# Sparse attention feeding a routed feed-forward layer: per-head-pair phases replaced by 128-query tiles over all heads, with a hand-written order

## The chip, the cores and the metric

The program runs on one core of a Trainium2 chip. A core has five engines that run at the same time and wait for each other through semaphores: TensorE (PE, matrix products; its weight loads are shown apart as PEld), VectorE (DVE), ScalarE (ACT), GpSimd (POOL) and SyncE (SP). Transfers between the large memory (DRAM) and the core's SBUF are issued by an engine's queue, here POOL and SP, and are carried out by 16 DMA engines. The metric is device time in microseconds (us) from the first to the last instruction; lower is better.

## What is computed

There are 4 batches, 8 heads, 768 positions and 64 values per head. Attention is sparse: a query sees the keys less than 16 positions away, and one summary for each of the 24 blocks of 32 keys (the maximum of the keys; the mean of the values). The heads' results stand side by side as 512 values per position. Then, for each batch, one of eight feed-forward experts is picked from the mean over positions, and only that expert's weights are used.

```python
k_sum = k.reshape(B, H, nb, 32, D).max(axis=3)
v_sum = v.reshape(B, H, nb, 32, D).mean(axis=3)
mask_l = np.abs(pos[:, None] - pos[None, :]) < 16
scores_s = scale * einsum('bhsd,bhnd->bhsn', q, k_sum) + np.log(32)
a = softmax(concat([where(mask_l, scale * q @ k.T, -1e9), scores_s]))
x = (a @ concat([v, v_sum])).transpose(0, 2, 1, 3).reshape(B, S, 512)
e_idx = argmax(x.mean(axis=1) @ w_gate, axis=1)
for e in range(8):
    mask = e_idx == e
    out[mask] = gate_w[mask] * (relu(x[mask] @ w1[e]) @ w2[e])
```

## The kernel before

Queries are taken in 12 blocks of 64 (`NJ`). A block needs 96 keys (its own 64 and 16 on either side) and the 24 summaries: 120 rows, which are the contraction of the second product. The work of a batch has these phases:

- `load_inputs(b)` (L75 to L121) issues the loads from POOL's queue: q and k in 128-position groups, 6 transfers each (L79, L83), alternating, and then v in overlapping windows of 96 rows, one transfer per head (L102). The overlap is read from DRAM again. Data is cast from float32 to bfloat16 on the way.
- `phase_T` (L245), for each of four head pairs: transposes of q and k on PE, the key blocks with their halos and block maxima on DVE (L260 to L285), sums of v over blocks on PE (L290), and a transfer on SP's queue that copies these sums into 24 rows of `vblk` for all 12 blocks (L301).
- `phase_S_head` (L308), for each head: scores (L321) into PSUM, exponential on ACT (L329), mask on DVE (L332), product with `vblk` (L339), reciprocal and scaling on DVE (L347, L348).
- `phase_X` (L355): transposes of the result; ACT's copy also adds up the positions for the gate (L359).
- The gate (L379 to L422): logits, the largest of eight, its index loaded into a register of POOL; then POOL issues the loads of that expert's weights, w1 in two halves (L426) and w2 in one piece (L433).
- The feed-forward of a batch (`moe_groups`, L177) is cut into 22 pieces: hidden layer by 128 features (L185, L199, relu L192, L206), output by 128 positions (L213, L221, written out at L222). They are handed out between the heads of the next batch.

The order in which an engine's instructions stand is chosen by a scheduler from priorities, within what the data allows; only the order of issue in the source guides it. The loads of batch b+1 are issued at the start of batch b (L240). On PE, ACT and DVE an instruction that waits holds up all behind it on that engine. PSUM has four pools of two banks each.

Of the kernel before, what the change touches and what calls it, by code (L numbers as in the profile page):

```python
# [12 lines left out]
FP32 = mybir.dt.float32  # L13
# [7 lines left out]

EMIT_ORDER = "T_all_first"
# [3 lines left out]
def kernel(  # L26
# [22 lines left out]
    NR = KW + NB  # L49
# [3 lines left out]
    NFT = F // 128  # L53
    SCALE = 1.0 / math.sqrt(D)
    KPAD = 16

    const_pool = ctx.enter_context(tc.tile_pool(name="const", bufs=1))

    ld_pool = ctx.enter_context(tc.tile_pool(name="ld", bufs=2))
    vb_pool = ctx.enter_context(tc.tile_pool(name="vb", bufs=2))  # L60
    pair_pool = ctx.enter_context(tc.tile_pool(name="pairp", bufs=6))
    head_pool = ctx.enter_context(tc.tile_pool(name="headp", bufs=8))
    xt_pool = ctx.enter_context(tc.tile_pool(name="xtp", bufs=2))
    moe_pool = ctx.enter_context(tc.tile_pool(name="moe", bufs=2))
    misc_pool = ctx.enter_context(tc.tile_pool(name="misc", bufs=2))

    tps_pool = ctx.enter_context(tc.tile_pool(name="tps", bufs=2, space=bass.MemoryType.PSUM))
    sc_pool = ctx.enter_context(tc.tile_pool(name="sc", bufs=2, space=bass.MemoryType.PSUM))
    ops_pool = ctx.enter_context(tc.tile_pool(name="ops", bufs=2, space=bass.MemoryType.PSUM))
    mps_pool = ctx.enter_context(tc.tile_pool(name="mps", bufs=2, space=bass.MemoryType.PSUM))  # L70


    v_off = v.offset

    def load_inputs(b):  # L75
        q_nat = ld_pool.tile([128, NG, H, D], BF16, name="q_nat")
        k_nat = ld_pool.tile([128, NG, H, D], BF16, name="k_nat")
        for g in range(NG):
            nc.gpsimd.dma_start(  # L79
                q_nat[:, g, :, :],  # L80
                q[b, :, g * 128 : (g + 1) * 128, :].rearrange("h p d -> p h d"),
            )
            nc.gpsimd.dma_start(  # L83
                k_nat[:, g, :, :],
                k[b, :, g * 128 : (g + 1) * 128, :].rearrange("h p d -> p h d"),
            )
        vblk = vb_pool.tile([NR, NP, NJ, 2, D + 1], BF16, name="vblk")
        nc.vector.memset(vblk[0:KW, :, :, :, D : D + 1], 1.0)
        for h in range(H):
            prc = h // 2  # L90
            hh = h % 2
            first_tensor_head = b == 0 and h == 0
            last_tensor_head = b == B - 1 and h == H - 1
            j_lo = 1 if first_tensor_head else 0
            j_hi = NJ - 1 if last_tensor_head else NJ
            base_elem = v_off + ((b * H + h) * S + (QB * j_lo - KPAD)) * D
            src = bass.AP(
                tensor=v.tensor,
                offset=base_elem,
                ap=[[D, KW], [QB * D, j_hi - j_lo], [1, D]],  # L100
            )
            nc.gpsimd.dma_start(vblk[0:KW, prc, j_lo:j_hi, hh, 0:D], src)  # L102
            if first_tensor_head:
                nc.gpsimd.dma_start(
                    vblk[KPAD:KW, prc, 0, hh, 0:D],
                    v[b, h, 0 : KW - KPAD, :],
                )
                nc.gpsimd.dma_start(
                    vblk[0:KPAD, prc, 0, hh, 0:D],
                    v[b, h, 0:KPAD, :],  # L110
                )
            if last_tensor_head:
                nc.gpsimd.dma_start(
                    vblk[0 : KW - KPAD, prc, NJ - 1, hh, 0:D],
                    v[b, h, S - (KW - KPAD) : S, :],
                )
# [355 lines left out]
```

## Time and profile before

| what | value |
|---|---|
| runs of the kernel, median (lowest to highest) | 242.04 us (241.69 to 242.19) |
| profiled execution: span from the first to the last instruction | 242.9 us |
| PE, DVE, ACT, POOL busy | 177.5, 105.9, 89.4, 85.6 us |
| first product on PE | at 21.4 us |
| loads of an expert's weights issued (four gates) | at 67.7, 115.1, 162.2 and 207.3 us |
| bytes read from and written to DRAM | 38.8 MB and 6.3 MB |

The profiled execution is known by its span alone; it lies 0.8 us above the median of the three runs. [...] A stage begins here where an expert's weights have landed and the hidden layer starts, since nothing of that batch's feed-forward can start before.

### The profile page before, as it was taken

The numbers are of one execution on the slowest core, as the hardware profiler recorded it, in microseconds if no ns is written. First come the engines' busy times: TensorE is split into PE (matmuls) and PEld (weight loads), VectorE is DVE, ScalarE is ACT, GpSimd is POOL, SyncE is SP. The second block draws the span as 40 slices with busy tenths as digits, with TensorE's granted clock in tenths as the row PEclk, the third lists the DMA queues.
The fourth block names the chain that finished last, engine by engine and source line by source line (L and its number), as shares of the span: only waits on it lengthen the run. The fifth ranks groups of instructions, "written<-read, shape, count | busy, mean of one in ns | idle before, by whom it ended". The sixth has DMA issues, their size and how long they took to land.

```text
span 242.9 us, 4351 instructions
## 1 busy us (share of the span) xinstructions
PE 177.5 (73%) x1712; PEld 106.2 (44%) x1712; DVE 105.9 (44%) x369; ACT 89.4 (37%) x193; POOL 85.6 (35%) x106
## 2 busy tenths in 40 slices
PE   0002257599959999788299999974999994098993
PEld 0002155477734555357145554652455443044441
DVE  1005999666597444028945340397354404000000
ACT  2000001463233465172045753800657437035432
POOL 8999999348185247016900000021000000300000
PEclk9999999655685999999869999997799998559999
DMA  8999999999969999939999504219900131793033
GB/s 52 149 132 96 126 145 129 106 125 137 114 102 186 152 103 148 212 135 109 160 171 137 17 3 167 91 31 185 170 15 0 46 149 68 101 186 61 0 131 130
DMA packets 104548, 27.18 MB, mean 112 GB/s; under 512 B 93264, under 2 KB 101456, under 8 KB 104528
## 3 DMA queue, kind: packets, MB, share of 16 engines
q0 software_dynamic: 95744, 19.40, 139.6%
q1 hardware_dynamic: 8784, 7.51, 11.8%
q8 instruction: 13, 0.21, 0.4%
q14 instruction: 7, 0.06, 0.1%
HBM read 38.81 MB, written 6.29 MB: 186 GB/s over the span
## 4 chain that ended last, share of the span: by engine, by line
PE 53%; DMA 19%; DVE 8%; POOL 8%; ACT 6%; issue 4%; POOLq 1%; ACTq 0%
PE hps L185 16%; PE hps L213 13%; DMA w_sb<-in_moe_w_dram 9%; PE hps L199 6%; PE sc L321 6%; PE ops L339 5%; DMA out_dram<-o_sb 5%; DMA vblk<-vsum_aug 5%; PE vsps L290 4%; POOL vblk L102 3%; ACT o_sb L221 2%; POOL q_nat L79 2%; POOL k_nat L83 2%; PE xps L358 2%; ACT hT_sb L192 1%
## 5 line engine op out<-in xcount | busy, mean ns | idle before, releaser
L185 PE MATMUL hps<-xT_b,w_sb 128*128 128x512 bf16 x128 | 41.3, 438 | 12.6 <-DMA w_sb<-in_moe_w_dram 11.4
L329 ACT ACTIVATE aT<-sc 128x512 bf16<-128x512 f32 x64 | 29.2, 490 | 51.6 <-PE sc L321 51.4
L213 PE MATMUL hps<-w_sb,hT_sb 128*128 128x512 bf16 x192 | 43.8, 379 | 2.1 <-ACT o_sb L221 1.9
L332 DVE TENSOR_TENSOR aT<-aT,mask_full 120x512 bf16<-120x512 bf16 x64 | 20.9, 346 | 52.3 <-ACT aT L329 52.2
L426 POOL DMA_DIRECT2D w_sb<-in_moe_w_dram x8 | 6.3, 791 | 91.3 <-DVE grec L410 83.3
L192 ACT ACTIVATE hT_sb<-hps 128x512 bf16<-128x512 f32 x32 | 19.1, 597 | 50.4 <-PE hps L185 50.4
L248 PE MATMUL qps<-identb,q_nat 128*128 128x128 bf16 x96 | 10.2, 246 | 32.3 <-POOL identb masks.py:199 21.4
L102 POOL DMA_DIRECT2D vblk<-in_v_dram x32 | 28.8, 938 | 12.0 <-PE ops L339 10.7
L213 PEld LDWEIGHTS <-hT_sb 128*128 128x128 bf16 x192 | 17.9, 98 | 23.0 <-issue 2.9
L221 ACT ACTIVATE o_sb<-hps,gcol 128x512 f32<-128x512 f32 x24 | 16.4, 688 | 28.8 <-PE hps L213 19.9
L321 PE MATMUL sc<-qT,kTaug 64*128 64x64 bf16 x384 | 23.1, 203 | 4.9 <-ACT aT L329 2.6
L83 POOL DMA_DIRECT2D k_nat<-in_k_dram x24 | 21.8, 907 | 13.3 <-DMA vblk<-in_v_dram 8.0
L79 POOL DMA_DIRECT2D q_nat<-in_q_dram x24 | 22.0, 918 | 7.2 <-DMA vblk<-in_v_dram 5.4
L321 PEld LDWEIGHTS <-kTaug 64*128 64x128 bf16 x384 | 16.4, 102 | 17.1 <-issue 15.0
L199 PE MATMUL hps<-xT_b,w_sb 128*128 128x256 bf16 x128 | 23.3, 298 | 0.0
L185 PEld LDWEIGHTS <-w_sb 128*128 128x128 bf16 x128 | 12.2, 107 | 23.9 <-DMA w_sb<-in_moe_w_dram 12.0
L248 PEld LDWEIGHTS <-q_nat 128*128 128x128 bf16 x96 | 7.2, 110 | 33.6 <-issue 27.8
L290 PE MATMUL vsps<-vblk,bindw 96*24 96x130 bf16 x192 | 18.7, 252 | 3.1 <-DVE bindw L174 2.6
L339 PE MATMUL ops<-vblk,aT 120*64 120x65 bf16 x384 | 16.6, 213 | 2.6 <-DMA vblk<-vsum_aug 1.5
L348 DVE TENSOR_TENSOR xs_pair<-ops,rv 128x384 bf16<-128x384 f32 x32 | 17.7, 554 | 0.4
L199 PEld LDWEIGHTS <-w_sb 128*128 128x128 bf16 x128 | 12.7, 107 | 9.5 <-issue 3.6
L339 PEld LDWEIGHTS <-aT 120*64 120x64 bf16 x384 | 11.4, 118 | 11.4 <-DVE aT L332 6.4
(69 smaller groups left out, 179.7 us busy)
## 6 DMA issues: line engine op xcount, KB each, us to landing
out_dram<-o_sb SPq DMA_DIRECT2D x24, 256.0 KB
vblk<-in_v_dram POOLq DMA_DIRECT2D x30, 144.0 KB, 8.2
w_sb<-in_moe_w_dram POOLq DMA_DIRECT2D x8, 512.0 KB, 6.6
w_sb<-in_moe_w_dram POOLq DMA_DIRECT2D x4, 1024.0 KB, 12.6
q_nat<-in_q_dram POOLq DMA_DIRECT2D x24, 128.0 KB, 6.0
k_nat<-in_k_dram POOLq DMA_DIRECT2D x24, 128.0 KB, 6.1
vblk<-vsum_aug SPq DMA_DIRECT2D x16, 73.1 KB
vblk<-in_v_dram POOLq DMA_DIRECT2D x2, 132.0 KB, 11.1
```

Source lines behind the costliest of these rows:

```text
L79: nc.gpsimd.dma_start(q_nat[:, g, :, :], q[b, :, g * 128 : (g + 1) * 128, :].rearrange("h p d -> p h d"),)
L83: nc.gpsimd.dma_start(k_nat[:, g, :, :], k[b, :, g * 128 : (g + 1) * 128, :].rearrange("h p d -> p h d"),)
L102: nc.gpsimd.dma_start(vblk[0:KW, prc, j_lo:j_hi, hh, 0:D], src)
L185: nc.tensor.matmul(hps1, lhsT=w1_sb[:, dt, ft * 128 : (ft + 1) * 128], rhs=xT_b[:, dt, 0:512], start=(dt == 0), stop=(dt == NDT - 1),)
L192: nc.scalar.activation(hT_sb[:, ft, 0:512], hps1, ACT.Relu)
L199: nc.tensor.matmul(hps2[:, 0 : S - 512], lhsT=w1_sb[:, dt, ft * 128 : (ft + 1) * 128], rhs=xT_b[:, dt, 512:S], start=(dt == 0), stop=(dt = ...
L213: nc.tensor.matmul(o_ps[:, 0:DM], lhsT=hT_sb[:, ft, st * 128 : (st + 1) * 128], rhs=w2_sb[:, ft, :], start=(ft == 0), stop=(ft == NFT - 1),)
L221: nc.scalar.activation(o_sb, o_ps[:, 0:DM], ACT.Copy, scale=gcol[:, 0:1])
L290: nc.tensor.matmul(vs_ps, lhsT=bindw[0:KW, j, :], rhs=vblk[0:KW, pr, j, :, :], start=(j == 0), stop=(j == NJ - 1),)
L321: nc.tensor.matmul(sc[0:128, cs], lhsT=kTaug[rs, j, :], rhs=qT[rs, QB * j : QB * (j + 1)], start=True, stop=True, tile_position=(hh * D, 0),)
L329: nc.scalar.activation(aT[:, j0 * QB : j1 * QB], sc[:, 0:ncols], ACT.Exp, scale=SCALE)
L339: nc.tensor.matmul(ops[(j % 2) * QB : (j % 2 + 1) * QB, j // 2, 0 : D + 1], lhsT=aT[0:NR, QB * j : QB * (j + 1)], rhs=vblk[0:NR, pr, j, hh ...
```

## The change

The kernel is written anew around tiles of 128 queries over all eight heads, and the scheduler is switched off: every engine's instructions stand as the source issues them. What differs:

- `vblk` and the key blocks `kaug` are two static tiles each, used in turn. v is loaded without overlap into 64 rows, two transfers of four heads each; the halo rows are copied from there by SP transfers (`halo`); the sums are copied into their 24 rows by DVE.
- Key blocks are made for all heads at once; the block maximum is a tree of DVE maxima, no longer one reduction.
- Scores, exponential, mask, second product and scaling are done for 128 queries and 8 heads in one go; one ACT instruction covers 1024 columns. Heads alternate between the upper and lower half of PE's rows.
- PSUM has two pools: two banks for transposes and three tiles of two banks (`big`) for everything else.
- w1 is loaded in four pieces, w2 in two; the hidden layer uses 384 columns per product.
- The order of loads, attention steps and feed-forward chunks is a list at the end. `weave` deals out steps among chunks.

```diff
-        vblk = vb_pool.tile([NR, NP, NJ, 2, D + 1], BF16, name="vblk")
...
-            nc.gpsimd.dma_start(vblk[0:KW, prc, j_lo:j_hi, hh, 0:D], src)
...
-    loaded = {0: load_inputs(0)}
-    identb = const_pool.tile([128, 128], BF16, name="identb")
-    make_identity(nc, identb)
...
+    ctx.enter_context(tc.manual_schedule())
...
+    tps_pool = ctx.enter_context(tc.tile_pool(name="tps", bufs=2, space=bass.MemoryType.PSUM))
+    big_pool = ctx.enter_context(tc.tile_pool(name="big", bufs=3, space=bass.MemoryType.PSUM))
...
+    def load_v(b):
+        vb = vblks[b % NV]
+        for a in range(2):
+            hs = slice(4 * a, 4 * a + 4)
+            nc.gpsimd.dma_start(
+                vb[0:QB, hs, :, 0:D].rearrange("p h j d -> p (h j) d"),
+                v[b, hs].rearrange("h (j p) d -> p (h j) d", p=QB),
+            )
+    def halo(b):
+        vb = vblks[b % NV]
+        for a in range(2):
+            hs = slice(4 * a, 4 * a + 4)
+            nc.sync.dma_start(
+                vb[R_PRE : R_PRE + HALO, hs, 1:NJ, :],
+                vb[QB - HALO : QB, hs, 0 : NJ - 1, :],
+            )
...
+    load_k(0)
+    identb = const.tile([128, 128], BF16, name="identb")
+    make_identity(nc, identb)
...
+    load_v(0)
+    load_q(0)
...
+    def V_sum(b):
+        def f():
...
+            for j in range(NJ):
+                for pr in range(NP):
+                    nc.tensor.matmul(
+                        vs_ps[BLK * pr : BLK * (pr + 1), :],
+                        lhsT=bind[:, j, :],
+                        rhs=vb[0:QB, 2 * pr : 2 * pr + 2, j, :],
...
+            nc.vector.tensor_copy(vs_sb.rearrange("p h c -> p (h c)"), vs_ps)
+            for pr in range(NP):
+                nc.vector.tensor_copy(
+                    vb[R_SUM:NR, 2 * pr : 2 * pr + 2, :, :],
...
+        for c in range(4):
+            fs = slice(c * (F // 4), (c + 1) * (F // 4))
+            nc.gpsimd.dma_start(w1_sb[:, :, fs], w1_src[:, :, fs])
...
+    def q_steps(b):
+        steps = [T_q(b, 0), T_q(b, 1)]
+        for g in range(NG + 2):
+            if g < NG:
+                steps.append(S_tile(b, g))
+            if g + 2 < NG:
+                steps.append(T_q(b, g + 2))
+            if 0 <= g - 1 < NG:
+                steps.append(O_tile(b, g - 1))
+            if 0 <= g - 2 < NG:
+                steps.append(X_tile(b, g - 2))
+        return steps
...
+    run(k_steps(0))
+    run(v_steps(0))
+    run(q_steps(0))
+    load_k(1)
+    edges(1)
+    gate(0)
+    load_v(1)
+    load_q(1)
+    load_k(2)
+    run(k_steps(1))
+    gate_col(0)()
+    weave(Hs(0), v_steps(1) + q_steps(1)[0:3])
+    weave(Os(0), q_steps(1)[3:])
+    gate(1)
+    load_v(2)
+    load_q(2)
+    load_k(3)
+    h1 = Hs(1)
+    weave(h1, k_steps(2) + v_steps(2) + q_steps(2)[0:3])
+    gate_col(1)()
+    weave(Os(1), q_steps(2)[3:])
+    load_v(3)
+    load_q(3)
+    gate(2)
+    weave(Hs(2), k_steps(3) + v_steps(3) + q_steps(3)[0:3])
+    gate_col(2)()
+    weave(Os(2)[0:6], q_steps(3)[3:])
+    gate(3)
+    run(Os(2)[6:])
+    gate_col(3)()
+    run(Hs(3))
+    run(Os(3))
```

`k_steps` are three `T_k` (transposes of k) and `K_rest` (halos, maxima); `T_q` transposes q, `S_tile` makes scores, exponential and mask, `O_tile` the second product and scaling, `X_tile` the transposes of the result and the sum over positions for the gate; `Hs` are the eight chunks of the hidden layer, `Os` the twelve half chunks of the output.

Three places show how instructions moved. The first is the start of POOL's queue in the kernel before; `L79` and `L83` are loads of q and k, `L102` of v (two small transfers for the first rows are left out).

```order
L83 DMA k_nat<-in_k_dram 128x8x64
L102 DMA vblk<-in_v_dram 96x11x64
...
L102 DMA vblk<-in_v_dram 96x12x64 x7
masks.py:197 MEMSET identb 128x128
L140 ISA
L140 IOTA it_u 96x768
masks.py:199 AFFINE_SELECT identb<-identb 128x128
```

In the changed kernel POOL's queue starts so (`L87` loads k or q, `L102` v).

```order
L87 DMA k_nat<-in_k_dram 128x8x64 x6
masks.py:197 MEMSET identb 128x128
masks.py:199 ISA
masks.py:199 AFFINE_SELECT identb<-identb 128x128
L124 IOTA it_u 96x64
L126 IOTA it_p 128x1
L128 IOTA it_b 64x384
L102 DMA vblk_84<-in_v_dram 64x48x64 x2
L87 DMA q_nat<-in_q_dram 128x8x64 x6
```

The identity, which every transpose needs, stood behind 12 loads of q and k and the ten transfers of v; it now stands behind the six loads of k, and v and q come after it.

The second place is POOL's queue at the first gate (`TENSOR_LOAD` waits for the expert's index). Before, v of batch 1, q and k of batch 2 and two heads of v of batch 2 stood ahead of it:

```order
L83 DMA k_nat<-in_k_dram 128x8x64
L102 DMA vblk<-in_v_dram 96x12x64 x2
L417 TENSOR_LOAD ix_691
L417 ISA x2
L426 ISA
L426 DMA w_sb<-in_moe_w_dram 128x4x512
...
L433 DMA w_sb<-in_moe_w_dram 128x8x512
L102 DMA vblk<-in_v_dram 96x12x64 x6
```

Now only k of batch 1 stands ahead of it, and v and q of batch 1 come behind the weights:

```order
L87 DMA k_nat<-in_k_dram 128x8x64 x6
L370 TENSOR_LOAD ix_601
L370 ISA x2
L383 ISA
L383 DMA w_sb<-in_moe_w_dram 128x4x256
...
L386 DMA w_sb<-in_moe_w_dram 128x4x512
L102 DMA vblk_85<-in_v_dram 64x48x64 x2
L87 DMA q_nat<-in_q_dram 128x8x64 x6
L87 DMA k_nat<-in_k_dram 128x8x64 x6
```

What moved is the load of v and q of the next batch: from ahead of the gate's wait to behind the weights. At the second gate it stands the same way; ahead of the third gate v and q of batch 3 are already issued.

The third place is on PE, where the sums of v over blocks stand. Before (`L290`, here those of batch 2), they lie among the transposes of q and k (`L248`, `L256`) around the gate's own products (`L412`), ahead of the hidden layer:

```order
L290 LDWEIGHTS bindw
L290 MATMUL vsps<-vblk,bindw 24x130
L248 LDWEIGHTS q_nat
L248 MATMUL qps<-identb,q_nat 128x128
...
L412 MATMUL gps<-grec,ones_row 128x1
L248 LDWEIGHTS q_nat
L248 MATMUL qps<-identb,q_nat 128x128
...
L185 LDWEIGHTS w_sb
L185 MATMUL hps<-xT_b,w_sb 128x512
```

In the changed kernel the sums of batch 1 (`L243`) stand behind the second of eight chunks of the hidden layer (`L424`) of batch 0:

```order
L424 MATMUL hps<-xT,w_sb 128x384
L243 LDWEIGHTS bind
L243 MATMUL vsps<-vblk_85,bind 32x132
...
L243 LDWEIGHTS bind
L243 MATMUL vsps<-vblk_85,bind 32x132
L424 LDWEIGHTS w_sb
L424 MATMUL hps<-xT,w_sb 128x384
```

Six chunks of the hidden layer, and everything after, now stand behind a product that needs v of the next batch.

## Rows read from the trace of the kernel before

**Rows 1.** The chain that ended last, in order of time: start, length, what.

```profile
36.80 11.35 DMA vblk<-vsum_aug
...
67.66 5.27 DMA w_sb<-in_moe_w_dram
...
115.05 6.21 DMA w_sb<-in_moe_w_dram
...
162.16 5.40 DMA w_sb<-in_moe_w_dram
...
207.29 5.39 DMA w_sb<-in_moe_w_dram
```

**Rows 2.** Timeline of the start: start, length, engine, line; idle time before, its end.

```profile
1.38 1.01 POOL L79 DMA_DIRECT2D q_nat<-in_q_dram  x1 [0.81 <-POOLq L456]
...
21.44 0.80 PE L248 MATMUL qps<-identb,q_nat 128*128 128x128 bf16 x6 [21.44 <-POOL identb masks.py:199]
```

**Rows 3.** Stretches: length; PE, PEld, DVE, ACT, POOL busy; clock, DMA, GB/s.

```profile
16.00:25.00 9.00, 1.44 (x12) 1.28 (x12) 3.82 (x4) 0.00 (x0) 9.00 (x14) 1.00 4.04 104
28.00:36.00 8.00, 4.62 (x41) 4.10 (x41) 7.94 (x23) 0.00 (x0) 8.00 (x10) 1.00 3.47 146
70.00:80.00 10.00, 8.41 (x56) 4.50 (x53) 7.54 (x29) 3.71 (x8) 6.15 (x8) 0.66 1.19 192
...
212.70:218.00 5.30, 5.27 (x17) 2.46 (x18) 0.00 (x0) 1.58 (x3) 0.00 (x0) 0.50 1.19 182
```

**Rows 4.** The chain again: its pieces on PE that give prices.

```profile
48.18 0.54 PE ops L339 x12
48.72 0.75 PE sc L321 x12
...
59.12 1.95 PE vsps L290 x17
...
86.58 0.35 PE ops L339 x12
...
89.05 0.44 PE hps L199 x4
...
108.33 0.44 PE xps L358 x6
...
228.17 10.53 PE hps L213 x48
```

**Rows 5.** Groups by line and shape: count, busy us, mean ns; idle before.

```profile
L79 POOL DMA_DIRECT2D q_nat<-in_q_dram x24 | 22.0, 918 | 7.2 <-DMA vblk<-in_v_dram 5.4 <-DMA w_sb<-in_moe_w_dram 0.9 <-POOLq L456 0.8
...
L348 DVE TENSOR_TENSOR xs_pair<-ops,rv 128x384 bf16<-128x384 f32 x32 | 17.7, 554 | 0.4
...
L266 DVE TENSOR_REDUCE kmx<-kTp 128x24 bf16<-128x768 bf16 x16 | 15.2, 947 | 0.0
...
L332 DVE TENSOR_TENSOR aT<-aT,mask_full 120x512 bf16<-120x512 bf16 x32 | 13.3, 414 | 50.1 <-ACT aT L329 49.9
L359 ACT ACTIVATE xT_b<-xps 128x768 bf16<-128x768 bf16 x16 | 12.9, 821 | 5.5 <-PE xps L358 5.3
...
L252 DVE COPY qT<-qps 128x768 bf16<-128x768 bf16 x16 | 8.4, 527 | 3.0 <-PE qps L248 3.0
L274 DVE COPY kTaug<-kTp 128x768 bf16<-128x768 bf16 x16 | 7.0, 436 | 0.0
...
L347 DVE RECIPROCAL rv<-ops 128x6 f32<-128x6 f32 x32 | 6.3, 196 | 17.5 <-PE ops L339 17.3
L281 DVE COPY kTaug<-kmx 128x288 bf16<-128x288 bf16 x16 | 5.5, 346 | 0.0
```

**Rows 6.** Timeline of the last gate, and of the end of the wait for weights.

```profile
205.41 0.15 DVE L396 COPY lg<-lgps 1x8 f32<-1x8 f32 x1 [0.29 <-PE lgps L394]
...
207.29 1.49 POOL L426 DMA_DIRECT2D w_sb<-in_moe_w_dram  x2 [42.36 <-DVE grec L410]
...
212.73 0.61 PE L185 MATMUL hps<-xT_b,w_sb 128*128 128x512 bf16 x1 [5.42 <-DMA w_sb<-in_moe_w_dram]
```

More of the change, by code (lines that the diff above doesn't have):

```diff
@@ L42 @@
     F = moe_w1.shape[2]
-    assert D == 64 and S % 128 == 0 and H % 2 == 0
+    assert D == 64 and S == 768 and H == 8
     QB = 64
-    KW = 96
+    HALO = 16
     BLK = 32
@@ new lines, with gate @@
+    gcols = {}
+    wts = {}
+    def gate(b):
+        pooled = small.tile([128, NP], FP32, name="pooled")
+        nc.vector.tensor_reduce(out=pooled, in_=red[b], axis=AX.X, op=ALU.add)
+        lgps = tps_pool.tile([128, 512], FP32, name="lgps", tag="tps")
+        for pr in range(NP):
+            nc.tensor.matmul(
+                lgps[0:1, 0:E],
+                lhsT=pooled[:, pr : pr + 1],
+                rhs=wg_sb[:, pr, :],
+                start=(pr == 0),
+                stop=(pr == NP - 1),
+            )
+        lg = small.tile([1, E], FP32, name="lg")
@@ new lines, in gate @@
+        for c in range(2):
+            fs = slice(c * (NFT // 2), (c + 1) * (NFT // 2))
+            nc.gpsimd.dma_start(w2_sb[:, fs, :], w2_src[:, fs, :])
+        negm = small.tile([1, 1], FP32, name="negm")
+        nc.vector.tensor_scalar(
+            out=negm, in0=mx8[0:1, 0:1], scalar1=-1.0 / S, scalar2=None, op0=ALU.mult
+        )
+        ex8 = small.tile([1, E], FP32, name="ex8")
+        se = small.tile([1, 1], FP32, name="se")
+        nc.scalar.activation(
+            out=ex8, in_=lg, func=ACT.Exp, bias=negm[0:1, 0:1], scale=1.0 / S, accum_out=se
+        )
@@ new lines, with H_chunk, f @@
+    hTs = {}
+    o_open = {}
+    def H_chunk(b, ft):
+        def f():
+            if ft == 0:
+                hTs[b] = xpool.tile([128, NFT, S], BF16, name="hT")
+            w1_sb = wts[b][0]
+            hps = big_pool.tile([128, 2, 512], FP32, name="hps", tag="big")
+            for half in range(2):
+                for dt in range(NDT):
+                    nc.tensor.matmul(
+                        hps[:, half, 0:HB],
+                        lhsT=w1_sb[:, dt, ft * 128 : (ft + 1) * 128],
+                        rhs=xT[b][:, dt, half * HB : (half + 1) * HB],
+                        start=(dt == 0),
+                        stop=(dt == NDT - 1),
+                    )
+            nc.scalar.activation(
+                hTs[b][:, ft, :].rearrange("p (u s) -> p u s", u=2),
+                hps[:, :, 0:HB],
+                ACT.Relu,
+            )
+        return f
@@ new lines, in O_chunk, with f @@
+    def O_chunk(b, st, part):
+        def f():
+            w2_sb = wts[b][1]
+            if part == 0:
+                o_open[b] = big_pool.tile([128, 2, 512], FP32, name="ops2", tag="big")
+            o_ps = o_open[b][:, 0, :]
+            for ft in range(4 * part, 4 * part + 4):
+                nc.tensor.matmul(
+                    o_ps,
+                    lhsT=hTs[b][:, ft, st * 128 : (st + 1) * 128],
+                    rhs=w2_sb[:, ft, :],
+                    start=(ft == 0),
+                    stop=(ft == NFT - 1),
+                )
+            if part == 1:
+                o_sb = opool.tile([128, DM], FP32, name="o_sb")
+                nc.scalar.activation(o_sb, o_ps, ACT.Copy, scale=gcols[b][:, 0:1])
+                nc.sync.dma_start(out[b, st * 128 : (st + 1) * 128, :], o_sb)
+        return f
@@ new lines, in run, with weave @@
+    def run(steps):
+        for s in steps:
+            s()
+    def weave(main, fill):
+        n, m = len(main), len(fill)
+        done = 0
+        for i, s in enumerate(main):
+            s()
+            want = (m * (i + 1)) // n
+            while done < want:
+                fill[done]()
+                done += 1
+    run(k_steps(0))
[8 more added lines that the diff above has]
+    run(k_steps(1))
```

562 lines of the change are left out of this document (242 added, 320 removed).

## Prediction

> **What bounds the kernel now.** I read the chain of waits first. It names the end of one wait per batch, the landing of that batch's expert weights, at 72.93, 121.26, 167.56 and 212.68 us (start plus length in [rows 1]). I cut the span of 242.9 us there: a start of 72.9, stages of 48.3, 46.3 and 45.1, and an end of 30.2. The chain also shows what made the start long: 11.35 us until the sums of v had been copied to their place, so that the first second product ran at 48.18 ([rows 1, 4]). The timeline says why it began late at all: POOL issues from 1.38 us, but PE's first transpose is at 21.44 and waited for the identity, which stands behind 22 loads on POOL ([rows 2]). At the other end, from the logits to the issue of the weights is 1.9 us and from the issue to the first product 5.4 ([rows 6]).
>
> The stretches give the transfer rates, counted as bfloat16 is written (an expert is 2.1 MB, v, q or k of a batch 0.79 MB). While v of batch 0 is moved, into 96 partitions, it is 104 GB/s; while q and k are, into 128, it is 146 with POOL issuing all the time; weights come at 182 to 192 ([rows 3]). Weights and v go through one queue in order, so these times add up.
>
> **The start.** POOL: 1.38 us and six loads of k at 0.9 ([rows 2, 5]) end at 6.8. Identity and three small iotas stand in no row of that size; nothing is the lower bound, the four instructions at 1 us each (as one load issue) the upper; I take 2.3, to 9.1. Then v. Its fixed part, from issue to first use, is what the first half of w1 needs beyond its 512 KB at 192 GB/s: 5.4 less 2.7 is 2.7 ([rows 3, 6]). The bytes take 5.4 us at the rate of q and k, 7.6 at that of v before; the new transfer writes 64 partitions where v wrote 96, so the nearer row is v's: 7.6, landed at 19.4. The 48 products of sums: halves of the array that take turns cost 45 ns each at half clock (12 in 0.54), the old sums 115 (17 in 1.95) ([rows 4]); so 2.2 to 5.5 us, I take 3.0, since here too four parts of the array take turns. DVE's cast and four copies of 1,584 elements, at the 0.57 ns of `L274` or the 1.2 ns of `L281` ([rows 5]), are 0.9 to 1.9 each; I take 1.0, since they run along rows of 66 values and not, as `L281`, across, and 0.3 for the small cast: 4.3 in all. With q's copy, 0.4, the first scores are at 27.1.
>
> A tile then costs DVE a mask of 1,024 (0.75, bounds 0.70 to 0.83 from `L348`, `L332`), q's copy of 512 (0.37), reciprocal (0.20), scaling of 512 (0.74) and the sum over positions of 512 (0.63, `L266`): 2.69 us, against 1.5 of PE and some 1.6 of ACT (`L359` at 1,024) ([rows 5]). Six are 16.1, with 4 until the first and after the last 20: 47.1. Edges for the second pair of tiles and the gate, 3.4 (1.9 of it read in [rows 6]): weights issued at **50.5**, before at 67.66. The first quarter of w1 needs 5.4 less 256 KB at 192 GB/s, 4.1: the hidden layer starts at 54.6. **Start: 18.3 us won.**
>
> **Stage 1.** Times from the issue. Before, the transposes and sums of the next batch filled the wait for weights, and its v had landed. Now v(1) is queued behind 2.1 MB: 2.7 + 10.9 + 7.6 = 21.2 us. PE has two chunks of the hidden layer in front of the sums, done by 9.5 even at half clock ([rows 3]), and then stands for 11 to 12 us; the six other chunks stand behind. After that: sums 3.0; six chunks of eight products of 384 columns, at 0.165 us (between 0.11 for 256 columns and 0.219 for 512 in [rows 4]) 7.9; half clock after the wait 1.0; a transpose and a score step 1.2: 34.3. Output woven with five and a half tiles: 10.5 of output, 8.5 of attention (per tile 32 products at 30 ns, from 0.35 for 12, and eight transposes at 73, from 0.44 for six; [rows 4]), and 2.0 for waits on PSUM: 21.0, to 55.3. Copy, sum, gate 4.1: next issue at 59.4. Before it was 48.3. **11.1 lost.**
>
> **Stage 2.** The sums stand behind five chunks and k's transposes, so PE has work until 15.0 and waits until the same 21.2. Sums 3.0, three chunks, transposes, scores and half clock 5.7, woven output 21.0, gate 4.1: 55.0 against 46.3. **8.7 lost.**
>
> **Stage 3.** v(3) and q(3) are issued ahead of the gate and land in the stage before. Hidden layer 10.6, k's transposes 1.75, sums 2.0, steps 1.2, half clock 2.5: 18.1. Only half the output is woven here (5.25 + 8.5 of PE), so DVE's 16.1 decides. Gate 4.1; the 4.1 of waiting for weights is covered by the other half of the output but still stands between the batches: 42.4 against 45.1. **2.7 won.**
>
> **End.** Hidden products began at 212.73 and output products at 228.17 ([rows 4, 6]), 15.4 us for 10.6 of products, which stopped for their two PSUM buffers; the output ends at 238.70, and 4.2 remain for the last copy and write. With three tiles of two banks I take 10.6 + 1.3 of half clock: 10.6 + 1.3 + 10.5 + 0.2 + 4.2 = 26.8. **3.4 won.**
>
> Sum: -18.3 + 11.1 + 8.7 - 2.7 - 3.4 = -4.6, a span of 238.3. The profiled execution lies 0.8 above the median of runs; the same taken off gives **237.5**. Reading v without overlap (64 rows a block, not 96) is in its bytes; the SP transfers of halos cost nothing: the halos are needed by the second product alone, behind sums and scores. If v landed later they would be late with it, already counted.
>
> **The rivals.** *Forecast (40%)*: v at 104 GB/s, 231 to 243. The price of v stands three times in the sum (start, stages 1 and 2), and a v slower by 1.5 us, 9.1 us or 86 GB/s, makes the change worth nothing.
>
> *Slower: the rate goes with the partitions written (25%).* 128 give 146 GB/s, 96 give 104 ([rows 3]); in the same ratio 64 give 69, v takes 11.4 us, three times 3.8 more: 249. For it speaks that the fall from 128 to 96 is about that steep; against it that both stretches have POOL busy throughout, so issue may set the rate, and the new load has two thirds of the pieces.
> [...]
>
> *Faster: issue sets the rate (20%).* Then v, as many pieces as q or k, comes at 146 GB/s, 5.4 us, 2.2 less three times; and the sums run at 45 ns a product, 0.8 less three times: 229. POOL's full stretches speak for it; the slower v before, under the same condition, against it.
>
> *Slower or even: three PSUM tiles for everything (15%).* Scores, second products, hidden, output and sums share `big`; one output holds a tile for two chunks. An exponential of 1,024 columns plus a second product's scaling hold the other two for about 2 us per tile. If each woven step waits, 2 to 5 us come onto each of three weaves, 243 to 252; from 1.5 us a weave the gain is gone. Before, four pools of two banks kept these apart, and DVE's mask already waited 49.9 us on ACT ([rows 5]).
>
> **How the numbers follow.** The likeliest case gives 237.5. Its own range, 231 to 243, is the bounds of copies and sums (the start's terms at their ends give -3 to +7, seldom all on one side) and 1 us of weave each way. All of it, the lower rival but its tail, and about half of each slower one lie in 225 to 250. A measurement of this kernel tells about 0.2%, 0.5 us, from no change. Faster: 35 of the forecast's 40, all 20 of the faster rival, 1 of the others, 56%; even 5%; slower 39%.
>
> **What would show it.** First scores near 27 us and weights issued near 50; else the start is wrong. At the first sums of batch 1, PE idle about 11 us with v named, at those of batch 2 about 6, none at batch 3; a wait of 15 is the slower rival, of 9 the faster. Stages near 59, 55, 42 and an end near 27. Waits of PE for scores' or second products' tiles inside the weaves, above 2 us in each, would show the PSUM rival. I am wrong if v is hidden, that is, if weights take so long that the sums' wait ends at another transfer, or if DVE's maxima and copies of k's blocks, which I gave nothing in stages 1 and 2 because PE waits for v there, end last.

## The result and the profile after

The changed kernel takes 228.83 us (median of four runs, 226.98 to 231.53) beside 242.12 for the kernel before; the ratio is 0.9415 (95% interval 0.935 to 0.948). It lies in the range of 225 to 250, on the side that was forecast, but below the likeliest case's own 231 to 243: 13.3 us were won and not 4.6. The profiled execution spans 227.3 us, where the sum gave 238.3.

The timeline of POOL after, its four issues of an expert's weights (start, length, line, idle time before them):

```profile
45.61 2.98 POOL L383 DMA_DIRECT2D w_sb<-in_moe_w_dram  x4 [21.69 <-DVE kaug L200]
...
102.07 2.98 POOL L383 DMA_DIRECT2D w_sb<-in_moe_w_dram  x4 [29.94 <-DVE grec L397]
...
155.76 2.99 POOL L383 DMA_DIRECT2D w_sb<-in_moe_w_dram  x4 [17.01 <-DVE grec L397]
...
195.72 2.97 POOL L383 DMA_DIRECT2D w_sb<-in_moe_w_dram  x4 [35.49 <-DVE grec L397]
```

These answer to the weights' transfers in [rows 1]. Cut at them, the prediction's terms stand so (us; the first row from the span's start, the last to its end):

| from, to | predicted | measured | difference |
|---|---|---|---|
| start to first weights | 50.5 | 45.6 | -4.9 |
| first to second | 59.4 | 56.5 | -2.9 |
| second to third | 55.0 | 53.7 | -1.3 |
| third to fourth | 42.4 | 40.0 | -2.4 |
| fourth to end | 30.9 | 31.6 | +0.7 |

Beside the kernel before, cut as in the prediction where the hidden layer starts (here at 49.7, 106.3, 159.8 and 201.0 us), the start won 23.2 us (18.3 predicted), stages 1 and 2 lost 8.3 and 7.2 (11.1 and 8.7), and stage 3 and the end won 3.9 each (2.7 and 3.4).

The chain that ended last, its long pieces (start, length, what):

```profile
9.33 9.13 DMA vblk<-in_v_dram
...
19.11 8.66 DMA vblk<-vblk
...
51.38 15.44 DMA vblk<-in_v_dram
66.87 1.50 PE vsps L243 x44
...
78.72 0.32 PE ops L445
...
107.84 15.41 DMA vblk<-in_v_dram
...
132.34 0.32 PE ops L445
...
169.79 0.80 PE vsps L243 x48
```

Where [rows 1] had the landing of weights, two stages now have the landing of v, 21.2 us after the issue of the weights both times (66.82 less 45.61; 123.25 less 102.07), which is what was predicted to a tenth. That the tenth fits is luck: the last of the weights landed 10.6 us after its issue at 49.3, which is 14.3 after the first issue where the sum had 13.6, and v took 6.9 more where it had 7.6; in stage 2 the two are the same. On the timeline of POOL, the wait for these weights in front of a load of q ends soon after:

```profile
60.48 0.88 POOL L87 DMA_DIRECT2D q_nat<-in_q_dram  x1 [2.00 <-DMA w_sb<-in_moe_w_dram]
```

New in the start is a piece that the prediction had put at nothing: 8.66 us of halo transfers.

The timeline of PE around the sums of batches 0, 1, 2 and 3 and the first scores (last bracket: idle time before, and what ended it):

```profile
18.51 1.50 PE L243 MATMUL vsps<-vblk,bind 64*32 64x132 bf16 x46 [3.38 <-DMA vblk<-in_v_dram]
...
23.94 0.61 PE L284 MATMUL sc<-qT,kaug 64*128 64x64 bf16 x16 [2.97 <-DVE qT L271]
...
63.52 0.29 PE L243 MATMUL vsps<-vblk,bind 64*32 64x132 bf16 x2 [8.62 <-DMA vblk<-in_v_dram]
66.87 1.50 PE L243 MATMUL vsps<-vblk,bind 64*32 64x132 bf16 x46 [3.06 <-DMA vblk<-in_v_dram]
...
119.80 0.29 PE L243 MATMUL vsps<-vblk,bind 64*32 64x132 bf16 x2 [4.04 <-DMA vblk<-in_v_dram]
123.30 1.50 PE L243 MATMUL vsps<-vblk,bind 64*32 64x132 bf16 x46 [3.20 <-DMA vblk<-in_v_dram]
...
169.72 0.87 PE L243 MATMUL vsps<-vblk,bind 64*32 64x132 bf16 x48
```

PE stands for v 8.62 + 3.06 = 11.7 us in stage 1 and 4.04 + 3.20 = 7.2 in stage 2, predicted as 11 to 12 and about 6. The sums that stand behind v are 1.5 us for 46 products, 33 ns each, and 0.87 for all 48, 18 ns each, at the last batch, where the granted clock is 1.00.

A tile of the start on VectorE, and the first instruction of the next (columns as before):

```profile
30.00 0.69 DVE L300 TENSOR_TENSOR aT<-aT,mask 120x1024 bf16<-120x1024 bf16 x1 [0.67 <-ACT aT L294]
30.60 0.42 DVE L271 COPY qT<-qps 128x512 bf16<-128x512 bf16 x1
30.94 0.20 DVE L324 RECIPROCAL rv<-ops 128x8 f32<-128x8 f32 x1
31.17 0.69 DVE L327 TENSOR_TENSOR xs<-ops,rv 128x512 bf16<-128x512 f32 x1
31.78 0.68 DVE L346 TENSOR_REDUCE red<-xT 128x4 f32<-128x512 bf16 x1
32.37 0.68 DVE L300 TENSOR_TENSOR aT<-aT,mask 120x1024 bf16<-120x1024 bf16 x1
```

The five durations add up to 2.68 us, the 2.69 of the prediction. But the next tile begins 2.37 us after this one: all but the scaling (`L327`) start while the instruction before is still recorded as running.

### The profile page after: what moved, and what is told of

Read it like the earlier page. It is cut to its first block, busy times and chain, and to the rows that moved or that the text cites. A ratio compares the mean times of both kernels' runs of the same rounds, so it can differ in the third digit from the quotient of the medians.

```text
span 227.3 us, 4141 instructions
## 1 busy us (share of the span) xinstructions
PE 151.1 (66%) x1721; PEld 90.8 (40%) x1736; DVE 103.5 (46%) x240; ACT 81.8 (36%) x113; POOL 72.5 (32%) x89
## 4 chain that ended last, share of the span: by engine, by line
PE 30%; DMA 29%; DVE 15%; ACT 8%; issue 8%; POOL 6%; POOLq 2%; SPq 0%; ACTq 0%
DMA vblk<-in_v_dram 18%; PE hps L424 12%; PE ops L445 11%; DMA w_sb<-in_moe_w_dram 8%; DVE aT L300 4%; DVE xs L327 4%; ACT aT L294 4%; DMA vblk<-vblk 4%; DVE red L346 3%; ACT o_sb L454 2%; POOL k_nat L87 2%; POOL vblk L102 2%; PE vsps L243 2%; PE ops L316 2%; POOL w_sb L383 1%
## 5 line engine op out<-in xcount | busy, mean ns | idle before, releaser
L424 PE MATMUL hps<-xT,w_sb 128*128 128x384 bf16 x256 | 54.2, 371 | 15.0 <-DMA w_sb<-in_moe_w_dram 14.9
L431 ACT ACTIVATE hT<-hps 128x768 bf16<-128x768 f32 x32 | 26.0, 811 | 72.0 <-PE hps L424 72.0
L445 PE MATMUL ops<-w_sb,hT 128*128 128x512 bf16 x177 | 47.0, 391 | 2.4 <-issue 0.8
L424 PEld LDWEIGHTS <-w_sb 128*128 128x128 bf16 x256 | 26.8, 109 | 35.4 <-DMA w_sb<-in_moe_w_dram 15.7
L294 ACT ACTIVATE aT<-sc 128x1024 bf16<-128x1024 f32 x24 | 24.5, 1021 | 26.7 <-PE sc L284 26.6
L87 POOL DMA_DIRECT2D k_nat<-in_k_dram x24 | 21.3, 898 | 14.5 <-DMA vblk<-in_v_dram 11.7
L300 DVE TENSOR_TENSOR aT<-aT,mask 120x1024 bf16<-120x1024 bf16 x24 | 16.6, 690 | 20.3 <-ACT aT L294 20.2
L445 PEld LDWEIGHTS <-hT 128*128 128x128 bf16 x192 | 17.3, 99 | 18.6 <-issue 2.9
L87 POOL DMA_DIRECT2D q_nat<-in_q_dram x24 | 21.4, 927 | 7.6 <-DMA w_sb<-in_moe_w_dram 6.6
L454 ACT ACTIVATE o_sb<-ops,gcol 128x512 f32<-128x512 f32 x24 | 16.5, 687 | 18.7 <-PE ops L445 17.0
L243 PE MATMUL vsps<-vblk,bind 64*32 64x132 bf16 x192 | 6.2, 286 | 24.3 <-DMA vblk<-in_v_dram 24.3
L345 ACT COPY xT<-xps 128x512 bf16<-128x512 bf16 x24 | 14.0, 585 | 13.8 <-PE xps L343 13.6
L346 DVE TENSOR_REDUCE red<-xT 128x4 f32<-128x512 bf16 x24 | 16.3, 682 | 3.6 <-ACT xT L345 3.6
L327 DVE TENSOR_TENSOR xs<-ops,rv 128x512 bf16<-128x512 f32 x24 | 16.6, 692 | 0.8
L243 PEld LDWEIGHTS <-bind 64*32 64x32 bf16 x192 | 4.9, 126 | 26.3 <-issue 21.8
## 6 DMA issues: line engine op xcount, KB each, us to landing
w_sb<-in_moe_w_dram POOLq DMA_DIRECT2D x8, 512.0 KB, 10.6
```

The costliest lines, as they stand in the source:

```text
L87: nc.gpsimd.dma_start(t[:, g, :, :], src[b, :, g * 128 : (g + 1) * 128, :].rearrange("h p d -> p h d"),)
L243: nc.tensor.matmul(vs_ps[BLK * pr : BLK * (pr + 1), :], lhsT=bind[:, j, :], rhs=vb[0:QB, 2 * pr : 2 * pr + 2, j, :], start=(j == 0), stop= ...
L294: nc.scalar.activation(aT.rearrange("p n c -> p (n c)"), sc.rearrange("p h c -> p (h c)"), ACT.Exp, scale=SCALE,)
L300: nc.vector.tensor_tensor(out=aT[0:NR], in0=aT[0:NR], in1=mask_b, op=ALU.mult)
L327: nc.vector.tensor_tensor(out=xs.rearrange("p r h d -> p h r d"), in0=ops[:, :, :, 0:D], in1=rv.unsqueeze(3).to_broadcast([128, 2, NP, D]) ...
L346: nc.vector.tensor_reduce(out=red[b][:, :, g], in_=dst, axis=AX.X, op=ALU.add)
```

## The experiments

Each is the changed kernel with one edit, unless said otherwise; ratios are to the kernel before on the same chip.

**v and q ahead of the gate** (`vq_ahead`).

```diff
     load_k(1)
+    load_v(1)
+    load_q(1)
     edges(1)
     gate(0)
-    load_v(1)
-    load_q(1)
     load_k(2)
+    load_v(2)
+    load_q(2)
...
     gate(1)
-    load_v(2)
-    load_q(2)
```

> v and q of the next batch are issued ahead of the gate's register load instead of behind the weights. Theory: TensorE's waits for v at the sums of batches 1 and 2 (11.7 and 7.2 us in the changed kernel) sit on the path, and go with the half clock after them: 19 to 21 us less than the changed kernel, near 209, no wait named v at these sums. Rival: the path behind them is held by VectorE, ScalarE and the weights as well, so half comes back there: near 219.

Measured: 206.03 us, ratio 0.847 (0.840 to 0.854), 22.8 less than the changed kernel. PE's sums of batches 1 and 2 have no wait in front:

```profile
56.50 0.87 PE L243 MATMUL vsps<-vblk,bind 64*32 64x132 bf16 x48
...
103.51 0.87 PE L243 MATMUL vsps<-vblk,bind 64*32 64x132 bf16 x48
```

The theory held, with 2 us more than it named; the next weights are issued 42.8 and 44.7 us after the last instead of 56.5 and 53.7. The place of v and q in POOL's queue costs the change more than the whole of what it wins.

**Only v ahead** (`v_ahead`): the same without the lines on q.

```diff
     load_k(1)
+    load_v(1)
     edges(1)
     gate(0)
-    load_v(1)
     load_q(1)
     load_k(2)
+    load_v(2)
...
     gate(1)
-    load_v(2)
     load_q(2)
```

> Only v moves ahead of the gate's load; q of the next batch stays behind the weights. Theory (the wait is one of queue order): q now lands at 2.7 + 10.9 + 5.4 = 19 us after the weights' issue, TensorE waits there instead, and only some 3 us per stage are won: near 223. Rival (it is v's own slow transfer): nearly all is won, near 211.

Measured: 209.41 us, ratio 0.863 (0.856 to 0.870). The rival's number came, but not its reason: q is late, yet at batch 1 PE waits for it 1.61 us in place of the 11.7 for v.

```profile
62.35 0.40 PE L266 MATMUL qps<-identb,q_nat 128*128 128x128 bf16 x4 [1.61 <-DMA q_nat<-in_q_dram]
```

My 19 us were those of the last of q's six pieces. A transpose needs only its own piece, and PE has the first 15.9 us after the weights' issue (46.5); all but the first two products of the sums need both pieces of v. So a load that is used piece by piece behind the weights costs little here, and one that is needed whole costs most of the wait.

**One column group for the sums** (`vsum_one_group`).

```diff
-            for j in range(NJ):
-                for pr in range(NP):
+            for pr in range(NP):
+                for j in range(NJ):
                     nc.tensor.matmul(
-                        vs_ps[BLK * pr : BLK * (pr + 1), :],
+                        vs_raw[0:BLK, pr // 2, (pr % 2) * 2 * DP : (pr % 2 + 1) * 2 * DP],
...
```

> The 48 products of a batch's sums all go to one group of 32 columns of the array instead of taking turns over four. Theory: the four groups run side by side, so one group costs 110 to 115 ns a product at half clock in place of 33: about 3.8 us more at each of the first three sums, 2 at the fourth, near 241 us. Rival: turns make no difference, a product is short by itself: 229.

The cast behind the sums then has 528 values in each of 32 rows, where it had 132 in each of 128.

Measured: 232.98 us, ratio 0.960 (0.950 to 0.969), 4.2 more, between the theory's 241 and the rival's 229. PE's sums of batches 0 and 1:

```profile
14.86 2.80 PE L242 MATMUL vsps<-vblk,bind 64*32 64x132 bf16 x24 [2.06 <-DMA vblk<-in_v_dram]
...
63.83 2.79 PE L242 MATMUL vsps<-vblk,bind 64*32 64x132 bf16 x24 [9.71 <-DMA vblk<-in_v_dram]
67.21 2.79 PE L242 MATMUL vsps<-vblk,bind 64*32 64x132 bf16 x24 [0.59 <-DMA vblk<-in_v_dram]
```

The price came as expected, 117 ns a product (2.80 for 24) against 33 (1.50 for 46): the four groups do run side by side. The total did not: one group needs the head pairs one after the other, so that half of the products now run before the second piece of v has landed; only 24 stand behind it, 1.3 us more per sum in place of 3.8 (the wider cast takes 0.70 us in place of 0.29). In the start nothing of this is left, since the wait for halos goes: weights are issued at 45.4 in place of 45.6. The stages from weights to weights are 2.0, 1.1 and 1.6 longer.

**The identity late** (`ident_late`).

```diff
     load_k(0)
-    identb = const.tile([128, 128], BF16, name="identb")
-    make_identity(nc, identb)
...
     load_v(0)
     load_q(0)
+    identb = const.tile([128, 128], BF16, name="identb")
+    make_identity(nc, identb)
```

> The identity is made behind all first loads again (k, v, q), as before the change; the rest is the changed kernel. Theory: the start then waits for v anyway, VectorE's work on k moves from 11 us to 16 and ends near 23, first scores near 27 in place of 24, of which 1 us was a wait for halos: 2 to 3 us slower, near 231. Rival: the identity was the start's bound and all 9 us by which it is later are paid: 238.

Measured: 230.91 us, ratio 0.947 (0.936 to 0.958), 2.1 more than the changed kernel, with intervals that overlap; its profile has the weights issued at 47.0 in place of 45.6, 1.4 later. PE's first scores:

```profile
26.66 0.61 PE L284 MATMUL sc<-qT,kaug 64*128 64x64 bf16 x16 [5.93 <-DVE qT L271]
```

As the theory had it: 2.7 us later scores, of which the wait for halos, now gone, gave back 1.1. The rival's 9 us are out.

**v behind q at the start** (`v_last`).

```diff
-    load_v(0)
     load_q(0)
+    load_v(0)
```

> The changed kernel with v of batch 0 loaded behind q in place of ahead of it. Theory (the start waits for v): v lands one load of q later, 5.3 us, and first scores and all behind come 4 to 5 us later, near 233. Rival: the halo transfers end last at the start (first second product waits for them until 27.8) and have less beside them now: within 1.5 us of the changed kernel.

Measured: 232.33 us, ratio 0.959 (0.954 to 0.964), 3.5 more, near the theory's 233, weights issued at 49.2. The start waits for v, so an early v matters there more than an early identity.

**The kernel before with the identity first** (`before_ident_first`).

```diff
-    loaded = {0: load_inputs(0)}
     identb = const_pool.tile([128, 128], BF16, name="identb")
     make_identity(nc, identb)
+    loaded = {0: load_inputs(0)}
```

> The kernel before, with the identity made ahead of all loads; nothing else of the change. Theory (the early identity is a good part of the start's gain): transposes start 12 us earlier, the sums of v then wait for v alone (landed near 25), their transfer starts near 30 in place of 36.8: about 8 us faster than before, near 234. Rival: in the old order v comes last and VectorE's transposes copies end no earlier than that, so the identity alone gives under 2 us: 240 to 242.

Measured: 253.98 us, ratio 1.052 (1.044 to 1.060): slower by 11 us, which neither theory had. PE's first transposes come at 5.0 us, but the sums of v wait for VectorE:

```profile
38.36 5.38 PE L290 MATMUL vsps<-vblk,bindw 96*24 96x130 bf16 x48 [11.74 <-DVE kTaug L285]
```

All 48 products of the sums now stand together behind VectorE's work on k (and, in the chain of waits, on the mask, `L148` and `L150`); [rows 1] had the sums' transfer at 36.80, here it starts at 40.19. That is 3.4 us; the first weights are issued 6.0 later than before, at 73.7, and the second 11.1 later, at 126.1, so most of the loss is not explained by it and stays open. The edit moved much of PE's order with it, so it does not price the identity; what the new order has in the start is identity and order together, and I leave their split in the old kernel open.

**No sum over positions** (`no_pos_sum`).

```diff
                 red[b] = small.tile([128, NP, NG], FP32, name="red")
+                nc.vector.memset(red[b], 0.0)
...
-            nc.vector.tensor_reduce(out=red[b][:, :, g], in_=dst, axis=AX.X, op=ALU.add)
```

> Leaves out the sum over positions for the gate on VectorE (24 reductions of 0.6 us; the pick is then among equal values); all else is the changed kernel. Theory (a tile costs what VectorE's instructions add up to, at the spacing of their starts, in the start and in stage 3): 6 x 0.6 = 3.5 us each there, nothing in stages 1 and 2, where TensorE is the bound: near 222. Rival (tiles are bound by the chain between engines or by PSUM tiles): under 2 us in all, near 227.

The 24 reductions are left out and zeros stand in their place. Measured: 220.83 us, ratio 0.913 (0.908 to 0.919), 8.0 less. The size is the theory's, the places are not: to the first weights and from weights to weights it is 43.1, 55.5, 51.4 and 38.1 (45.6, 56.5, 53.7, 40.0 in the changed kernel), so 2.5, 1.0, 2.3 and 1.9 less. The stretch after the wait for v is held by VectorE in part too, and no stretch wholly.

**The halo transfers at the start** (`k1_behind`).

```diff
-    load_k(1)
     edges(1)
     gate(0)
+    load_k(1)
     load_v(1)
```

> k of batch 1 is loaded behind the first weights, no longer beside the halo transfers of batch 0. Only the start is looked at: theory (halo transfers are slow because loads run beside them) the halos take 6 us or less in place of 8.7, the first second product runs near 26.4 without a wait, weights issued near 44.3 in place of 45.6. Rival: the halo transfer is slow by itself: no change at the start. Behind it k and v come later and the whole is slower, 240 to 250 us.

Measured, in a single run: second products begin at 25.57 without a wait for halos, and the weights are issued 2 us earlier.

```profile
20.31 2.31 DVE L253 COPY vblk<-vs_sb 24x1584 bf16<-24x1584 bf16 x4
...
25.57 0.78 PE L316 MATMUL ops<-vblk,aT 120*64 120x65 bf16 x16 [0.21 <-DVE aT L300]
...
43.61 2.98 POOL L383 DMA_DIRECT2D w_sb<-in_moe_w_dram  x4 [27.59 <-DVE grec L397]
```

Of the 2 us, 0.8 is there at the first scores already (23.12 in place of 23.94), since the four copies of the sums take 2.31 us in place of 3.06; the rest, some 1.2, is what the halos cost the changed kernel where I gave them nothing. The last halo transfer lands 6.7 us after its issue, not the 6 or less of the theory, in place of 8.7: k of batch 1 beside it accounts for 2 us, and most of its length is not due to k. The whole ran in 231.36 us, less slow than the 240 that I had expected.

**How many rows v is written to** (`probe_rows`), and **how far apart its pieces stand** (`probe_pitch`): extra loads of v of batch 0 into a tile that nobody reads, ahead of all others. The first writes 64 and then 128 rows:

```diff
+    scr = const.tile([128, 96, D], BF16, name="scr")
+    for p_ in (64, 128):
+        n_ = 4 * S // p_
+        for a in range(2):
+            nc.gpsimd.dma_start(
+                scr[0:p_, a * n_ : (a + 1) * n_, :],
+                v[0, 4 * a : 4 * a + 4].rearrange("h (j p) d -> p (h j) d", p=p_),
+            )
```

The second keeps 64 rows and varies the distance:

```diff
+    scr = const.tile([64, 96 * 80], BF16, name="scr")
+    for pitch in (64, 66, 72, 80):
+        view = scr[:, 0 : 96 * pitch].rearrange("p (n c) -> p n c", c=pitch)
+        for a in range(2):
+            nc.gpsimd.dma_start(
+                view[:, a * 48 : (a + 1) * 48, 0:D],
+                v[0, 4 * a : 4 * a + 4].rearrange("h (j p) d -> p (h j) d", p=64),
+            )
```

> Adds, ahead of all loads, v of batch 0 loaded twice into a scratch tile nobody reads: first as in the changed kernel into 64 rows (2 transfers of 64 x 48 x 64), then into 128 rows (2 of 128 x 24 x 64); same bytes and pieces, one after the other (load buffers two in place of three). By the partitions (64 rows half the rate of 128): 69 to 75 GB/s and then 146. By issue alone: 146 both times. By the landing of v in the changed kernel (0.79 MB in 6 to 7.6 us): 105 to 130 for 64 rows.

> Adds, ahead of all loads, v of batch 0 loaded four times into 64 rows of a scratch tile nobody reads, each after the one before has landed, with the pieces of 64 values (128 bytes) standing 64, 66, 72 and 80 values apart in a row (load buffers two in place of three). The tiles of v stand 66 apart, and while v goes there the trace shows 120 to 133 GB/s with the DMA engines' share at 4.3 to 5.0; the probe before, 64 apart, showed 141 to 153 at 2.2 to 2.4. Theory (the distance does it, not the number of rows): 64 as before; 66 shows 105 to 133 GB/s and a share over 4; 72 and 80 lie between or as 64. Rival (what lies beside it did it): all four alike, 140 to 155 at 2.2 to 2.5.

In the first, both stretches moved 151 to 155 GB/s, into 64 rows (5 to 9 us) and into 128 (11 to 13); one of each (last two columns: DMA share, GB/s):

```profile
5.00:6.00 1.00, 0.00 (x0) 0.00 (x0) 0.00 (x0) 0.00 (x0) 0.00 (x0) 1.00 2.42 155
11.00:12.00 1.00, 0.00 (x0) 0.00 (x0) 0.00 (x0) 0.00 (x0) 1.00 (x2) 1.00 2.41 154
```

In the second, the stretches for pieces 64 (to 10 us), 66 (13 to 20) and 72 apart (23 to 30):

```profile
5.00:6.00 1.00, 0.00 (x0) 0.00 (x0) 0.00 (x0) 0.00 (x0) 0.00 (x0) 1.00 2.45 157
14.00:15.00 1.00, 0.00 (x0) 0.00 (x0) 0.00 (x0) 0.00 (x0) 0.00 (x0) 1.00 2.37 151
17.00:18.00 1.00, 0.00 (x0) 0.00 (x0) 0.00 (x0) 0.00 (x0) 0.00 (x0) 1.00 4.67 124
18.00:19.00 1.00, 0.00 (x0) 0.00 (x0) 0.00 (x0) 0.00 (x0) 0.00 (x0) 1.00 4.43 110
24.00:25.00 1.00, 0.00 (x0) 0.00 (x0) 0.00 (x0) 0.00 (x0) 0.00 (x0) 1.00 2.31 148
28.00:29.00 1.00, 0.00 (x0) 0.00 (x0) 0.00 (x0) 0.00 (x0) 0.00 (x0) 1.00 3.92 112
```

The slow rate is not that of 64 rows. With 64 apart all is fast (141 to 157 GB/s in the full microseconds); with 66, the distance in `vblk`, the first half is as fast and the second falls to 110 to 124 GB/s; 72 is like 66, and 80 showed no such fall (153 to 157). Each is one execution, and why only the second half falls is open.

**Covering the waits for weights too** (`cover`, then `cover2`). Both load v and q ahead and put each gate ahead of the last half of the output before. `cover` puts the key steps, sums and two transposes of the next batch in a bunch ahead of the hidden layer:

```diff
...
+        weave(Hs(b), qs[2:11])
+        os_b = Os(b)
+        weave(os_b[0:4], qs[11:])
+        run(os_b[4:6])
+        gate(n)
...
+        run(os_b[6:])
+        if n + 1 < B:
+            run(k_steps(n + 1) + v_steps(n + 1) + q_steps(n + 1)[0:2])
+        gate_col(n)()
...
```

`cover2` weaves them:

```diff
...
+    for b in range(B - 1):
+        n = b + 1
+        qs = q_steps(n)
+        weave(Hs(b), v_steps(n) + qs[0:9])
+        gate_col(b)()
+        os_b = Os(b)
+        weave(os_b[0:6], qs[9:])
+        gate(n)
+        if n + 2 < B:
+            load(n + 2)
+        weave(os_b[6:], k_steps(n + 1) if n + 1 < B else [])
...
```

> As with v and q ahead (206 us), and the wait for weights is covered too: each gate stands ahead of the last half of the output before, and the key steps, the sums of v and two transposes of the next batch stand ahead of its hidden layer. Theory: TensorE's waits for weights (16.3 us in three stages) and most of the gates' (7.8) go, and with them some half clock: 186 to 192. Rival: VectorE's steps, now bunched in front of the hidden layer, make attention the bound, and under 8 us are won: 198 to 204.

> As with v and q ahead (206 us); each gate stands ahead of the last half of the output before, in whose six chunks the next batch's key steps are woven, and attention starts earlier among the hidden chunks; nothing stands ahead of the hidden layer but the key steps of batch 1. Theory: the waits for weights and gates of the second and third stage (together some 11 us of TensorE's idle time) are covered and VectorE's work is spread: 193 to 199. Rival: VectorE and ScalarE hold attention, the waits only move: 203 to 207.

`cover` measured 209.42 us, ratio 0.864 (0.858 to 0.870), nothing better than 206 and neither the theory's 186 to 192 nor the rival's 198 to 204. PE's largest wait by the list of waits (total, times, longest):

```profile
PE gps L403 <- DVE qT L271: 18.2, 3, 6.3
```

The product that spreads the gate's weight needs a PSUM tile which the bunched transposes hold until VectorE, busy with k and v, has copied them; the hidden layer is behind it on PE. `cover2` measured **193.08 us**, ratio 0.795 (0.788 to 0.802), better than both kernels and at the lower end of the theory's 193 to 199. From weights to weights it is 38.4, 38.2 and 37.5 us, and of the hidden layer's waits for weights only the first batch's, 4.6 us, is left:

```profile
PE hps L424 <- DMA w_sb<-in_moe_w_dram: 4.6, 1, 4.6
```

## Why the prediction was right in its mechanism and wrong in its size

- **The wait for v** was right: where it stands, that it appears twice and not a third time, PE idle 11.7 and 7.2 us. Its end 21.2 us after the issue of the weights was right by two errors of 0.7 that cancel. Undone with q's place, it gives 22.8 us, 3.9 more than the two waits.
- **The failed step is the price of v's 48 products**, "I take 3.0", 62 ns between rows at 45 and 115. Measured: 33 ns for three of the sums (granted clock 0.50 at batches 1 and 2; for batch 0 see the last section) and 18 for the last (1.00), 1.5 us and 0.87 (2.0 predicted), 1.1 to 1.5 less each time; even the lower bound of 2.2 was too high. It stands four times on the path, so some 5.6 of the 10.9 us by which the sum was off, the largest single term. The row at 45 ns was for two halves that take turns; four groups of 32 columns do better, and one group is 117. I had the reason in the text and still went away from the low end.
- **VectorE's time was added from durations.** 2.69 us a tile was right as a sum and 2.37 is what a tile costs. From first scores to last sum the start took 17.8 us, predicted 20, with 1.1 of a wait for halos in it; the four copies of sums cost 3.4 with the cast, predicted 4.3 (2.6 where POOL issues nothing, see below). In the rows above mask, scaling and sum are 0.68 to 0.69 us long, and the instruction behind each starts 0.59 to 0.61 after it. In the kernel before the same could be read, from starts instead of means; there the mask is 0.38 long and the next instruction starts 0.30 after it:

```profile
52.53 0.38 DVE L332 TENSOR_TENSOR aT<-aT,mask_full 120x512 bf16<-120x512 bf16 x1
52.83 0.55 DVE L348 TENSOR_TENSOR xs_pair<-ops,rv 128x384 bf16<-128x384 f32 x1
```

- **The load of v** was right as a sum: issued at 7.99 and landed at 18.46, 10.5 us against 2.7 + 7.6. POOL came to it 1.1 us earlier than the 9.1 predicted, since identity and iotas took 1.2 us in place of 2.3. The rival by rows is out: 64 rows were written at 151 to 155 GB/s with the pieces 64 apart, and at 118 to 148 in the changed kernel itself (66 apart, 13 to 18 us), where it had 69. The faster rival's reason for v is out as well: POOL's two issues take 2.72 us for what takes over 5 us to move even at 155 GB/s, so issue is not the bound.
- **The faster rival's number, 229, is what was measured**, but by luck and another way: its cheap sums, VectorE's spacing, and not its faster v.
- **PSUM** is out: inside the woven outputs PE waits 1.3 and 1.4 us in 20 by the list of waits, for VectorE's scaling and mask, where above 2 would have shown it. In stage 1:

```profile
PE xps L343 <- DVE xs L327: 0.6, 1, 0.6
...
PE ops L316 <- DVE aT L300: 0.4, 1, 0.4
...
PE ops L316 <- DVE xs L327: 0.3, 2, 0.2
```

- **The woven output and the gate**, 21.0 + 4.1 in the prediction, took 23.4 us from the first output product (78.72 and 132.34) to the next issue, 1.7 less in both stages. The 2.0 for waits on PSUM had no row behind it, and the list names none. In stage 3 the hidden layer and the steps woven into it, without the sums, are 1.1 shorter.
- **What came longer**: halos that "cost nothing" cost some 1.2 us at the start, inside the 17.8 above. In stage 2, from the sums' end to the first output product, it took 7.5 us in place of 5.7: the 24 products of the three chunks behind the wait took 6.2 us, where the prediction's 0.165 us a product makes 4.0. The end is 0.7 longer than predicted, the gate of the start 0.5; other terms are under 0.3.
- **Profile and runs**: a run's time is 1.6 to 1.7 us above its span wherever both are on record (228.99 beside 227.3 for the profiled execution after). So the profiled execution before, known by its span of 242.9, was some 2.5 us slower than the median of runs and not 0.8, and the one after 0.2. From span to span 15.6 us were won, from median to median 13.3, and 2.3 of the 10.9 by which the sum was off do not show in the median.

By these rows the cheap sums are 5.6 us, all else that came shorter adds up to some 8.7, and what came longer to some 3.5. What stays open is how the 8.7 share out between VectorE's spacing and TensorE in the later stages, since taking VectorE's reductions out moved all stages a little; and which part of the start's gain is the identity's.

## What to carry to other kernels

Price an instruction that stands back to back by the distance between starts (here 0.59 to 0.61 us on VectorE for 0.68 to 0.69 long), and small products by the group of the array that they use (33 ns in turns over four groups, 117 on one), not by the nearest row of another shape; such terms count once for each time they stand on the path. On a queue that is served in order, put every load that an engine needs whole ahead of the wait for a value: here that place was worth 19.4 us for v alone and 22.8 with q, more than the rewrite itself (13.3). To cover a wait, weave work in; bunched steps moved the wait here to another engine (`cover`, 18.2 us of PE waiting for VectorE; 209.42 us, woven 193.08).

## What the runs showed of the hardware

The windows of PE at three sums (after the length, PE busy and count; granted clock third from the end):

```profile
18.40:20.00 1.60, 1.49 (x47) 1.29 (x47) 0.00 (x0) 0.00 (x0) 1.05 (x2) 1.00 3.27 154
66.80:68.40 1.60, 1.53 (x47) 1.33 (x47) 0.00 (x0) 0.00 (x0) 1.29 (x2) 0.50 3.53 151
169.70:170.70 1.00, 1.00 (x51) 0.81 (x50) 0.93 (x3) 0.81 (x1) 0.00 (x0) 1.00 0.01 1
```

The row at 18.4 says a granted clock of 1.00, yet its 47 products take 1.49 us, as long as the 1.53 at 66.8 under 0.50 and near twice the 0.87 that 48 of them take at 169.7 under 1.00 (among 51 in that row). In the first stretch of this kernel the record of the clock can't be taken at its word; the products' durations tell it. That transfers slow the products there is out: the same stretch, almost without transfers, in the changed kernel and with the identity late (`ident_late`), where the record says 0.50, has as long products:

```profile
30.00:36.00 6.00, 5.60 (x114) 4.29 (x112) 5.90 (x13) 4.21 (x6) 0.00 (x0) 1.00 0.12 9
...
30.00:36.00 6.00, 5.67 (x112) 4.35 (x106) 5.82 (x14) 4.17 (x5) 0.00 (x0) 0.50 0.03 4
```

The four copies of the sums on VectorE have two prices in one kernel, here at batches 0 and 3:

```profile
20.37 3.06 DVE L253 COPY vblk<-vs_sb 24x1584 bf16<-24x1584 bf16 x4
...
171.72 2.31 DVE L253 COPY vblk<-vs_sb 24x1584 bf16<-24x1584 bf16 x4
```

At batch 0 POOL issues loads of k meanwhile (18.95 to 22.45 and 23.00 to 23.92 us), at batch 3 none. With nothing issued beside them they take 2.31 us at the start too (`k1_behind`). The fourth copy of batch 0 starts at 22.87, between two issues, and takes 0.57 us with transfers at 128 GB/s; the three ahead of it, which start during issues, take 0.72 to 0.87. So POOL's issuing, not the transfers, goes with the 0.75 us; no run here shows by what path.
